# Turning w, r and k for 16 of 24 attention units on VectorE instead of TensorE

## The chip, the core and the metric

The kernel runs on one core of a Trainium2 chip. The metric is the device time of one execution in microseconds. A core has five engines that run side by side and wait for each other by semaphores: TensorE (PE, with its weight loads PEld), VectorE (DVE), ScalarE (ACT), GpSimd (POOL) and SyncE (SP), which in this kernel issues all transfers. Each engine works through its own instructions in order.

## What is computed

A linear attention with a per-channel decay, then two feed-forward layers on all 3,072 tokens. B=4 batches, H=8 heads, S=768 time steps, D=48 channels a head, all float32; the feed-forward weights come as float64.

```python
for t in range(S):
    kt, vt, rt, wt = (k[:, :, t], v[:, :, t], r[:, :, t], w[:, :, t])
    cur = np.einsum('bhd,bhe->bhde', u[None] * kt, vt)
    y[:, :, t] = np.einsum('bhd,bhde->bhe', rt, state + cur)
    state = wt[:, :, :, None] * state + np.einsum('bhd,bhe->bhde', kt, vt)
# layer 1 (384 -> 2048 -> 384)
h = x @ w_in; g = h - np.tanh(h); x = g @ w_out
# layer 2 (384 -> 1024 -> 384)
h = x @ w_in; e = np.exp(h - max(h)); sm = e / (sum(e) + 1e-9); solu = h * sm
out = ((solu - mean) / sqrt(var + 1e-6) * g_ln) @ w_out
```

## The kernel before

The attention is cut into 24 units of 128 time steps (4 batches of 6), each for all 8 heads. A unit needs r, k and w with the channels in the partitions and the time along the columns: head pair j has its even head in partitions 0 to 47 and its odd head in 64 to 111, so that one tile of 128x4x128 (j, time) holds all heads. `att_load` (L182) reads them as they lie in memory, time in the partitions, in runs of 48 floats, into `rkw`, two buffers that units take in turn; v goes into one of four `vt`. `_transposes` (L216) turns one of the three with four 128x128 transposes on TensorE into a PSUM bank.

A unit has six parts. `att_pre` (L194): ScalarE tests w against its two bounds with sums into `flags` (L198, L200), GpSimd multiplies u, r and k (L202, L203), VectorE sums them over the channels (`dg`, L204). `att_0`: transposes of w and r (L219), the running product of w by four scans on VectorE (L228), its inverse by Ln and Exp on ScalarE (L231, L232), `rh` (L233). `att_1`: transposes of k, and `kh` out of it (L240 to L242). `att_2`: the products of r and k (`qk`), masked into `aq`, and `kh` turned back. `att_3`: the state, `ds` on TensorE and L281, L282 on VectorE. `att_4`: the output `y`, split into a rounded and a remaining half (L299 to L302, into `xs` and `x3`), and six small copies from `x3` into `xs` that SyncE issues (L305).

The first layer runs in 6 blocks of 512 tokens with 16 steps each, 96 steps in all. Each step s has `part1` (nine 128x512 matmuls into `hp`, L335; then L340 to L347 on ScalarE and VectorE, L351 and L352 on GpSimd, which make `g`) and, of the step two before, `part2` (nine matmuls from `g` into three banks `x2p`, L359). Part k of unit u is put into step 4u + k - 18, so four steps carry one unit, and the four units of a block are done two steps before the block begins. `att_pre` is in step 4u - 19 and `att_load` in step 4u - 24. The first four units run ahead of the steps. The weights are converted from float64 during the first steps, and later steps read them again to test them (`check_pair`). After the last steps the second layer runs over 24 tiles of 128 tokens; there VectorE already turns data in 32x32 blocks (L473).

A scheduler gives every engine's instructions their order, from readiness in a simulated run; the code above sets the priorities. Attention takes its PSUM from a pool of three banks with the tag "a" (`bank`, L206): for w, r, k, two for qk, kt, ds and y of every unit.

Of the kernel before, what the change touches and what calls it, by code (L numbers as in the profile page):

```python
# [20 lines left out]
C = 128  # L21
NC = S // C
# [8 lines left out]
NP = 112  # L31

# [23 lines left out]
class Kern:  # L56
# [101 lines left out]
    def att_setup(self, att, xp0, xp1):  # L158
        nc = self.nc
        self.rkw = [att.tile([128, 3, H, 64], F32, name=f"rkw{i}") for i in range(2)]  # L160
# [32 lines left out]

    def att_pre(self, u):  # L194
        nc = self.nc
        t = self.rkw[u % 2]
        w = t[:, 2, :, 0:D]
        nc.scalar.activation(self.ruk, w, AF.Relu, bias=self.c_lo, scale=-1.0,  # L198
                             accum_out=self.flags[:, 2 * u:2 * u + 1])
        nc.scalar.activation(self.ruk, w, AF.Relu, bias=self.c_hi,  # L200
                             accum_out=self.flags[:, 2 * u + 1:2 * u + 2])
        nc.gpsimd.tensor_tensor(self.ruk, t[:, 0, :, 0:D], self.ub, ALU.mult)  # L202
        nc.gpsimd.tensor_tensor(self.ruk, t[:, 1, :, 0:D], self.ruk, ALU.mult)  # L203
        nc.vector.reduce_sum(self.dg[u % 2].rearrange("p e j -> p j e"), self.ruk.rearrange("p (j e) d -> p j e d", e=2), axis=AX)  # L204
# [17 lines left out]
    def att_0(self, u):  # L222
        nc, v = self.nc, self.nc.vector
        inc = self.inc[u % 2]
        pw = self._transposes(u, 2)
        pr = self._transposes(u, 0)
        for j in range(4):
            v.tensor_tensor_scan(inc[:NP, j, 1:], pw[:NP, j], self.zeros[:NP].to_broadcast([NP, C]), 1.0, ALU.mult, ALU.add)  # L228
        full = inc[:NP, :, 1:]
        kh = self.kh[u % 2]  # L230
        nc.scalar.activation(kh[:NP], full, AF.Ln, bias=self.c_min[:NP])  # L231
        nc.scalar.activation(kh[:NP], kh[:NP], AF.Exp, scale=-1.0)  # L232
        v.tensor_tensor(self.rh[u % 2][:NP], pr[:NP], inc[:NP, :, 0:C], ALU.mult)  # L233

    def att_1(self, u):
# [3 lines left out]
        pk = self._transposes(u, 1)  # L239
        self.nc.gpsimd.tensor_tensor(inv, full, kh, ALU.mult)  # L240
        v.tensor_tensor(kh, kh, pk[:NP], ALU.mult)
        v.scalar_tensor_tensor(kh, inv, 2.0, kh, ALU.subtract, ALU.mult)  # L242
# [284 lines left out]
def fast_path(tc, K, const):  # L527
# [8 lines left out]
    K.st0 = const.tile([128, 40], F32, name="st0")  # L536
# [34 lines left out]
    for s in range(-2, NB * NM + 2):  # L571
# [10 lines left out]
        if rem == 0 and UB + 1 < u < NU:  # L582
            K.att_load(u)
        if 0 <= s - 2 < NB * NM:
# [12 lines left out]
        if s == LAST + NM - 2:  # L597
# [6 lines left out]
            hs = {0: K.b_h(K.load_x2(0), 0, None, (K.st0[:, 0:8], K.st0[:, 8:40], *big))}  # L604
# [222 lines left out]
```

## Time and profile before

| what | value |
|---|---|
| median of 3 runs | 807.62 us (806.01, 807.74, 807.62) |
| the profiled execution | 804.36 us |
| its span, first to last instruction | 802.6 us |
| TensorE busy | 755.1 us (94%) |
| VectorE, ScalarE, GpSimd busy | 559.0, 499.1, 423.8 us |
| moved by DMA | 97.40 MB, mean 121 GB/s |

A busy TensorE is not a TensorE at its peak: matmuls overlap, and their ends are modelled. What an instruction costs there is read from the starts of the ones behind it. Idle time of an engine matters only where something waits for it.

### The profile page before, as it was taken

The numbers are of one execution on the slowest core, as the hardware profiler recorded it, in microseconds if no ns is written. First come the engines' busy times: TensorE is split into PE (matmuls) and PEld (weight loads), VectorE is DVE, ScalarE is ACT, GpSimd is POOL, SyncE is SP. The second block draws the span as 40 slices with busy tenths as digits, with TensorE's granted clock in tenths as the row PEclk, the third lists the DMA queues.
The fourth block names the chain that finished last, engine by engine and source line by source line (L and its number), as shares of the span: only waits on it lengthen the run. The fifth ranks groups of instructions, "written<-read, shape, count | busy, mean of one in ns | idle before, by whom it ended". The sixth has DMA issues, their size and how long they took to land. (4 is left out here: it accounts for less than half of the span.)

```text
span 802.6 us, 13281 instructions
## 1 busy us (share of the span) xinstructions
PE 755.1 (94%) x4530; PEld 626.6 (78%) x4530; DVE 559.0 (70%) x975; ACT 499.1 (62%) x944; POOL 423.8 (53%) x388
## 2 busy tenths in 40 slices
PE   3777988999999999999999999999998999999997
PEld 2666766788888888888888888776877899898886
DVE  4678979875555555565556555468559999998882
ACT  3435777786677776676767664588735555454552
POOL 3544765655565565455565555366615445445440
PEclk9979999999999999999999999999999999999999
DMA  9965576563454645354354210033035555555521
GB/s 165 175 107 126 144 162 125 149 153 87 101 125 101 146 85 123 85 154 100 97 131 142 64 46 25 32 131 118 2 121 178 169 175 169 175 166 167 188 99 46
DMA packets 167150, 97.40 MB, mean 121 GB/s; under 512 B 109088, under 2 KB 155808, under 8 KB 167072
## 3 DMA queue, kind: packets, MB, share of 16 engines
q1 hardware_dynamic: 167072, 96.45, 47.6%
q8 instruction: 38, 0.62, 0.3%
q14 instruction: 40, 0.33, 0.1%
HBM read 73.08 MB, written 20.97 MB: 117 GB/s over the span
## 5 line engine op out<-in xcount | busy, mean ns | idle before, releaser
L335 PE MATMUL hp<-xs,wa 128*128 128x512 f32 x864 | 221.9, 397 | 6.2 <-DVE y L346 2.6
L359 PE MATMUL x2p<-g,wa 128*128 128x512 f32 x864 | 223.0, 397 | 4.7 <-POOL g L352 3.1
L335 PEld LDWEIGHTS hp<-xs,wa 128*128 128x128 f32 x864 | 160.3, 189 | 43.9 <-DVE y L346 3.5
L359 PEld LDWEIGHTS x2p<-g,wa 128*128 128x128 f32 x864 | 158.2, 188 | 41.5 <-POOL g L352 6.3
L352 POOL TENSOR_TENSOR g<-y,g 128x512 fp32r<-128x512 f32 x96 | 128.7, 1341 | 43.7 <-ACT g L349 30.0
L341 DVE TENSOR_TENSOR y<-hp,t 128x512 f32<-128x512 f32 x96 | 66.1, 689 | 101.9 <-ACT t L340 95.6
L420 PE MATMUL h<-wb,x2s 128*128 128x512 f32 x432 | 107.6, 403 | 2.4 <-POOL x2s L405 2.3
L498 PE MATMUL o<-wb,ts 128*128 128x384 f32 x576 | 106.4, 339 | 0.9 <-POOL ts L477 0.9
L347 ACT ACTIVATE q<-t,cst 128x512 f32<-128x512 f32 x96 | 69.4, 723 | 59.7 <-DVE y L346 59.2
L498 PEld LDWEIGHTS o<-wb,ts 128*128 128x128 f32 x576 | 101.9, 188 | 3.3 <-POOL ts L477 1.3
L420 PEld LDWEIGHTS h<-wb,x2s 128*128 128x128 f32 x432 | 82.0, 190 | 22.2 <-POOL x2s L405 3.3
L351 POOL TENSOR_SCALAR g<-y 128x512 fp32r<-128x512 f32 x64 | 44.2, 691 | 84.8 <-DVE y L346 84.1
L340 ACT ACTIVATE t<-hp 128x512 f32<-128x512 f32 x96 | 56.8, 591 | 42.2 <-PE hp L335 42.0
L477 POOL TENSOR_TENSOR ts<-tw,ts 128x512 fp32r<-128x512 f32 x44 | 55.8, 1291 | 4.8 <-ACT ts L476 4.7
L346 DVE SCALAR_TENSOR_TENSOR y<-q,y 128x512 f32<-128x512 f32 x64 | 53.3, 833 | 5.9 <-ACT q L344 2.1
L246 POOL TENSOR_SCALAR_AFFINE_SELECT aq<-dg 128x1024 f32<-128x1024 f32 x24 | 28.4, 1182 | 39.6 <-PE y L297 36.6
L405 POOL TENSOR_TENSOR x2s<-x2s 128x384 fp32r<-128x384 f32 x24 | 24.4, 1017 | 43.9 <-ACT x2s L404 43.9
L344 ACT ACTIVATE q<-t,cst 128x512 f32<-128x512 f32 x64 | 46.3, 724 | 1.8
L451 POOL TENSOR_TENSOR st<-st,cst 128x1 f32<-128x1 f32 x24 | 13.2, 551 | 64.1 <-DVE st L450 47.4
L449 ACT ACTIVATE e<-so 128x1024 f32<-128x1024 f32 x24 | 25.4, 1059 | 33.6 <-DVE so L448 33.5
L473 DVE STREAM_TRANSPOSE tw<-sw 128x1024 f32<-128x1024 f32 x22 | 45.3, 2058 | 1.2 <-issue 0.4
L219 PE MATMUL tp<-ident,rkw 128*128 128x128 f32 x264 | 40.7, 290 | 5.7 <-DMA rkw<-in_w_dram 5.6
(120 smaller groups left out, 1218.4 us busy)
## 6 DMA issues: line engine op xcount, KB each, us to landing
raw<-in_moe_w_out_dram SPq DMA_DIRECT2D x48, 384.0 KB, 3.9
dso<-so SPq DMA_DIRECT2D x22, 512.0 KB, 3.0
sw<-dso SPq DMA_DIRECT2D x88, 128.0 KB, 3.0
raw<-in_moe_w_in_dram SPq DMA_DIRECT2D x64, 144.0 KB, 3.2
raw<-in_moe_w_in_dram SPq DMA_DIRECT2D x16, 384.0 KB, 3.2
rkw<-in_w_dram SPq DMA_DIRECT2D x24, 192.0 KB, 4.2
rkw<-in_r_dram SPq DMA_DIRECT2D x24, 192.0 KB, 4.6
rkw<-in_k_dram SPq DMA_DIRECT2D x24, 192.0 KB, 4.1
```

The costliest lines, as they stand in the source:

```text
L335: self.mm(hp, self.wa[:, a, m, j * 128:(j + 1) * 128], xs[:, b, j], start=n == 0, stop=n == len(seq) - 1)
L340: nc.scalar.activation(t, hp, AF.Square)
L341: v.tensor_tensor(y, hp, t, ALU.mult)
L344: nc.scalar.activation(p, t, AF.Square, bias=self.c_fsb, scale=F_S)
L346: self.last_dve = v.scalar_tensor_tensor(y, p, F_E, y, ALU.add, ALU.mult)
L347: self.last_act = nc.scalar.activation(q, t, AF.Relu, bias=self.c_t2, accum_out=self.flags[:, col:col + 1])
L352: g.tensor_tensor(gs[:, 1], y, gs[:, 0], ALU.subtract)
L359: self.mm(self.x2p[d], self.wa[:, a, m, sl], gs[:, b], start=m == 0 and n == 0, stop=m == NM - 1 and n == 2)
L420: self.mm(p[:, f], xs[:, a, j], w, start=q == 0, stop=q == 8)
L473: self.turned = nc.vector.transpose(x.rearrange("p k (t b) -> p b k t", b=4), sw)
L477: nc.gpsimd.tensor_tensor(ts[:, 1, k], x[:, k], ts[:, 0, k], ALU.subtract)
L498: self.mm(p, ts[:, a, k], self.wb[:, b, k, DM:], start=q == 0, stop=q == 3 * NM2 - 1)
```

## The change

From unit 8 on (TURN = 2 x UB = 8; sixteen of 24 units), w, r and k are not transposed on TensorE. `load_grp` reads each in groups of four consecutive time steps (192 floats, 768 bytes in one run) into a block buffer `grp`, with four copies of 32 partitions: partition 32g + t holds time steps 4t to 4t + 3 of every head of one parity, and the second of two groups of partitions stands 32 columns further left, so that the same column range shows channels 0 to 31 in one and 32 to 47 (with 16 unused) in the other. `turn` then lets VectorE transpose 32x32 blocks out of it into a PSUM bank, writing every fourth column, which gives the layout that the transposes gave. The block buffers are single and lie, together with a natural copy of r and k (`nat`, for `att_pre`), in the place of the two `rkw` buffers; each overlaps the next by 32 columns. `load_turned` takes the place of `att_load`, in step 4u - 21, with 15 issues in place of 4. The test of w moves from `att_pre` to `att_0` and reads the turned w in PSUM (128x512 in place of 128x384). In `att_1` an intermediate goes to the bank of k in place of `kh`. The small tile `st0` is dropped, and `ub` serves in its place.

```diff
--- before.py
+++ after.py
@@ -29,6 +29,9 @@
 NM2 = FF2 // 128
 NTT = NT // 128
 NP = 112
+RKW = 3 * H * 64
+ROW = 4 * 4 * D
+TURN = 2 * UB
 
 
 W_LO, W_HI = 0.75, 1.34
@@ -157,7 +160,10 @@
 
     def att_setup(self, att, xp0, xp1):
         nc = self.nc
-        self.rkw = [att.tile([128, 3, H, 64], F32, name=f"rkw{i}") for i in range(2)]
+        rkw = att.tile([128, 2 * 3 * H * 64 + 32], F32, name="rkw")
+        self.rkw = [x.rearrange("p (i h d) -> p i h d", i=3, h=H) for x in (rkw[:, 0:RKW], rkw[:, RKW:2 * RKW])]
+        self.grp = [rkw[:, ROW * i:ROW * (i + 1) + 32] for i in range(3)]
+        self.nat = rkw[:, 3 * ROW + 32:2 * RKW + 32].rearrange("p (i h d) -> p i h d", i=2, h=H)
         self.vt = [att.tile([128, DM], F32, name=f"vt{i}") for i in range(4)]
         self.inc = [att.tile([128, 4, C + 1], F32, name=f"inc{i}") for i in range(2)]
         self.rh = [att.tile([128, 4, C], F32, name=f"rh{i}") for i in range(2)]
@@ -191,16 +197,51 @@
             in_=self.v[b, :, sl, :].rearrange("h p d -> p h d"),
         )
 
+    def load_grp(self, i, u):
+        b, c = divmod(u, NC)
+        x = (self.k, self.r, self.w)[i][b].rearrange("(j e) (c t x) d -> e c t j (x d)", e=2, c=NC, x=4)
+        for g in range(4):
+            e, half = divmod(g, 2)
+            o = 32 - 32 * half
+            self.nc.sync.dma_start(
+                out=self.grp[i][32 * g:32 * g + 32, o:o + ROW].rearrange("p (j n) -> p j n", j=4), in_=x[e, c]
+            )
+
+    def load_turned(self, u):
+        nc = self.nc
+        b, c = divmod(u, NC)
+        sl = slice(c * C, (c + 1) * C)
+        if u == TURN:
+            nc.gpsimd.memset(self.grp[2][:, ROW:], 1.0)
+        self.load_grp(2, u)
+        self.load_grp(1, u)
+        for i, src in ((0, self.r), (1, self.k)):
+            nc.sync.dma_start(out=self.nat[:, i], in_=src[b, :, sl, :].rearrange("h p d -> p h d"))
+        nc.sync.dma_start(
+            out=self.vt[u % 4].rearrange("p (h d) -> p h d", h=H),
+            in_=self.v[b, :, sl, :].rearrange("h p d -> p h d"),
+        )
+        self.load_grp(0, u)
+
+    def turn(self, u, i):
+        p = self.bank(u, "tp")
+        x = self.grp[i][:, 32:32 + ROW].rearrange("p (j x c) -> p j x c", j=4, x=4)[:, :, :, 0:32]
+        self.nc.vector.transpose(p.rearrange("p j (t x) -> p j x t", x=4), x)
+        return p
+
+    def check_w(self, u, w, tmp):
+        for i, (b, s) in enumerate(((self.c_lo, -1.0), (self.c_hi, 1.0))):
+            self.nc.scalar.activation(tmp, w, AF.Relu, bias=b, scale=s,
+                                      accum_out=self.flags[:, 2 * u + i:2 * u + i + 1])
+
     def att_pre(self, u):
         nc = self.nc
         t = self.rkw[u % 2]
-        w = t[:, 2, :, 0:D]
-        nc.scalar.activation(self.ruk, w, AF.Relu, bias=self.c_lo, scale=-1.0,
-                             accum_out=self.flags[:, 2 * u:2 * u + 1])
-        nc.scalar.activation(self.ruk, w, AF.Relu, bias=self.c_hi,
-                             accum_out=self.flags[:, 2 * u + 1:2 * u + 2])
-        nc.gpsimd.tensor_tensor(self.ruk, t[:, 0, :, 0:D], self.ub, ALU.mult)
-        nc.gpsimd.tensor_tensor(self.ruk, t[:, 1, :, 0:D], self.ruk, ALU.mult)
+        r, k = (t[:, 0, :, 0:D], t[:, 1, :, 0:D]) if u < TURN else (self.nat[:, 0], self.nat[:, 1])
+        if u < TURN:
+            self.check_w(u, t[:, 2, :, 0:D], self.ruk)
+        nc.gpsimd.tensor_tensor(self.ruk, r, self.ub, ALU.mult)
+        nc.gpsimd.tensor_tensor(self.ruk, k, self.ruk, ALU.mult)
         nc.vector.reduce_sum(self.dg[u % 2].rearrange("p e j -> p j e"), self.ruk.rearrange("p (j e) d -> p j e d", e=2), axis=AX)
 
     def bank(self, u, name):
@@ -222,8 +263,13 @@
     def att_0(self, u):
         nc, v = self.nc, self.nc.vector
         inc = self.inc[u % 2]
-        pw = self._transposes(u, 2)
-        pr = self._transposes(u, 0)
+        if u < TURN:
+            pw = self._transposes(u, 2)
+            pr = self._transposes(u, 0)
+        else:
+            pw = self.turn(u, 2)
+            self.check_w(u, pw, self.kh[u % 2])
+            pr = self.turn(u, 1)
         for j in range(4):
             v.tensor_tensor_scan(inc[:NP, j, 1:], pw[:NP, j], self.zeros[:NP].to_broadcast([NP, C]), 1.0, ALU.mult, ALU.add)
         full = inc[:NP, :, 1:]
@@ -236,10 +282,10 @@
         v = self.nc.vector
         kh, inv = self.kh[u % 2][:NP], self.inv[:NP]
         full = self.inc[u % 2][:NP, :, 1:]
-        pk = self._transposes(u, 1)
+        pk = self._transposes(u, 1) if u < TURN else self.turn(u, 0)
         self.nc.gpsimd.tensor_tensor(inv, full, kh, ALU.mult)
-        v.tensor_tensor(kh, kh, pk[:NP], ALU.mult)
-        v.scalar_tensor_tensor(kh, inv, 2.0, kh, ALU.subtract, ALU.mult)
+        v.tensor_tensor(pk[:NP], kh, pk[:NP], ALU.mult)
+        v.scalar_tensor_tensor(kh, inv, 2.0, pk[:NP], ALU.subtract, ALU.mult)
 
     def att_2(self, u):
         nc, v = self.nc, self.nc.vector
@@ -533,7 +579,6 @@
     K.load_act_set()
     K.setup(const)
     K.gl = const.tile([128, NM2], F32, name="gl")
-    K.st0 = const.tile([128, 40], F32, name="st0")
     L, R, R2 = ExitStack(), ExitStack(), ExitStack()
     cv = pool(L, "cv", 2)
     cvr = pool(L, "cvr", 2)
@@ -579,8 +624,11 @@
         if rem == 0 and UB < u < NU:
             K.att_pre(u)
         u, rem = divmod(s - OFF + 6, 4)
-        if rem == 0 and UB + 1 < u < NU:
+        if rem == 0 and UB + 1 < u < TURN:
             K.att_load(u)
+        u, rem = divmod(s - OFF + 3, 4)
+        if rem == 0 and TURN <= u < NU:
+            K.load_turned(u)
         if 0 <= s - 2 < NB * NM:
             K.part2(*divmod(s - 2, NM), gs.pop(s - 2))
         if 0 <= s < NM - early:
@@ -601,7 +649,8 @@
                 for x in ("e0", "so0")
             ]
             K.ps_b, K.exps = (ps_r,), []
-            hs = {0: K.b_h(K.load_x2(0), 0, None, (K.st0[:, 0:8], K.st0[:, 8:40], *big))}
+            small = K.ub.rearrange("p h d -> p (h d)")
+            hs = {0: K.b_h(K.load_x2(0), 0, None, (small[:, 0:8], small[:, 8:40], *big))}
         n, due = divmod(3 * (s - NM), 7)
         if 0 <= n < NM + NM2 and due < 3:
             K.check_pair(cvr, n)
```

## Rows read from the trace of the kernel before

**Rows 1.** The page: busy time of TensorE, its 40 slices, its granted clock

```profile
PE 755.1 (94%) x4530; PEld 626.6 (78%) x4530; DVE 559.0 (70%) x975; ACT 499.1 (62%) x944; POOL 423.8 (53%) x388
...
PE   3777988999999999999999999999998999999997
...
PEclk9979999999999999999999999999999999999999
```

**Rows 2.** Stretches: length, busy PE, PEld, DVE, ACT, POOL (count), clock, DMA share, GB/s

```profile
259.10:280.40 21.30, 21.30 (x138) 17.22 (x137) 12.01 (x23) 15.92 (x33) 12.55 (x12) 1.00 0.62 154
...
302.50:324.60 22.10, 22.10 (x154) 18.10 (x153) 13.28 (x25) 15.49 (x31) 12.90 (x12) 1.00 0.52 109
...
sum 343.30, PE 343.30 PEld 281.23 DVE 203.72 ACT 237.12 POOL 198.94; mean PE 21.46 PEld 17.58 DVE 12.73 ACT 14.82 POOL 12.43
```

**Rows 3.** Timeline of TensorE in one unit: start us, us, instruction, count

```profile
307.01 1.09 PE L219 MATMUL tp<-ident,rkw 128*128 128x128 f32 x8
307.86 2.32 PE L359 MATMUL x2p<-g,wa 128*128 128x512 f32 x9
310.02 2.26 PE L335 MATMUL hp<-xs,wa 128*128 128x512 f32 x9
...
313.04 0.60 PE L219 MATMUL tp<-ident,rkw 128*128 128x128 f32 x4
313.39 1.40 PE L359 MATMUL x2p<-g,wa 128*128 128x512 f32 x5
...
322.51 2.22 PE L359 MATMUL x2p<-g,wa 128*128 128x512 f32 x9
```

**Rows 4.** Groups by line, whole run: busy us, mean ns, idle us before

```profile
L219 PE MATMUL tp<-ident,rkw 128*128 128x128 f32 x264 | 40.7, 290 | 5.7 <-DMA rkw<-in_w_dram 5.6
```

**Rows 5.** Timeline of GpSimd in the same unit

```profile
307.17 1.25 POOL L246 TENSOR_SCALAR_AFFINE_SELECT aq<-dg 128x1024 f32<-128x1024 f32 x1 [2.30 <-PE y L297]
...
316.48 1.29 POOL L352 TENSOR_TENSOR g<-y,g 128x512 fp32r<-128x512 f32 x1
```

**Rows 6.** The stretch of that unit, L219 alone

```profile
302.50:324.60 22.10, 1.69 (x12) 1.36 (x12) 1.00 0.52 109
```

**Rows 7.** Two lines of VectorE: ns shortest/median/longest, first and last start

```profile
L473 DVE STREAM_TRANSPOSE tw<-sw x22: 2024/2060/2067, 602.8 to 778.4; 128x1024 f32<-128x1024 f32 x22
...
L346 DVE SCALAR_TENSOR_TENSOR y<-q,y x64: 667/692/1583, 167.1 to 508.7; 128x512 f32<-128x512 f32 x64
```

**Rows 8.** Timeline of VectorE in the same unit; idle time before in brackets

```profile
305.36 0.74 DVE L281 TENSOR_TENSOR st<-ds,st 48x192 f32<-48x192 f32 x2 [2.64 <-PE ds L272]
...
307.50 1.47 DVE L346 SCALAR_TENSOR_TENSOR y<-q,y 128x512 f32<-128x512 f32 x1
...
314.02 0.69 DVE L241 TENSOR_TENSOR kh<-kh,tp 112x512 f32<-112x512 f32 x1
```

**Rows 9.** A check of w on ScalarE, 155 to 499 us: ns shortest/median/longest

```profile
L200 ACT ACTIVATE inv<-rkw,cst x15: 601/616/618, 164.0 to 469.2; 128x384 f32<-128x384 f32 x15
```

**Rows 10.** Groups by line: a 128x512 operation of ScalarE with a sum

```profile
L347 ACT ACTIVATE q<-t,cst 128x512 f32<-128x512 f32 x96 | 69.4, 723 | 59.7 <-DVE y L346 59.2
```

**Rows 11.** Timeline of SyncE's issues, in that unit and ahead of 424 us

```profile
310.95 3.78 SPq L305 DMA_DIRECT2D xs<-x  x6
...
317.45 0.42 SPq L320 DMA_DIRECT2D raw<-in_moe_w_out_dram  x1
...
419.25 3.99 SPq L305 DMA_DIRECT2D xs<-x  x6
```

**Rows 12.** Transfers, whole run: count, KB each, median us to landing

```profile
rkw<-in_r_dram SPq DMA_DIRECT2D x24, 192.0 KB, 4.6
```

**Rows 13.** Landing of the six x3 copies issued from 419.25 us

```profile
DMA to landing us min/median/max: 1.8/1.8/3.0
```

**Rows 14.** Timeline of TensorE at the border of 424 us

```profile
426.17 1.09 PE L335 MATMUL hp<-xs,wa 128*128 128x512 f32 x4
```

**Rows 15.** SyncE's waits, 120 to 500 us: total us, times, longest us

```profile
SPq L315 <- ACT raw L138: 44.4, 10, 7.6
```

## The prediction

> **What bounds the kernel now.** I read the page's engine totals and slices first, then a table of stretches over the steps that the change touches, then the order of instructions of one attention unit on each engine, and last the queue of SyncE and the transfers.
>
> The totals put TensorE at 94% and the slices show it full from the eighth slice on, at full clock [rows 1]. The table of stretches says it more sharply: from 155.3 us, where unit nine (index 8) begins to be transposed, to 498.6 us, TensorE is busy for 343.30 of 343.30 us at a granted clock of 1.00, while VectorE has 203.72, ScalarE 237.12 and GpSimd 198.94 us of work [rows 2]. These are the sixteen units that change. In this stretch an instruction taken off TensorE shortens the time unless something else then ends last; one added to another engine costs nothing while its chain has room.
>
> One unit takes 22.1 us. In the order of TensorE [rows 3] its w and r transposes (L219, eight of them) start at 307.01 and the next matmul at 307.86: 0.85 us. The four of k start at 313.04, the next matmul at 313.39: 0.35 us. They are pipelined, so the spacing of the starts is what they cost, 0.10 us each; the mean of 290 ns in the grouped line [rows 4] is latency and overlaps.
>
> How much room have the others? The chain of a step runs from hp (L335) over ScalarE, VectorE (L341, L346) and GpSimd (L351, L352) to part2 (L359), which TensorE runs about two steps later. In the unit shown the tightest of four is that of hp at 310.02: its g is ready at 316.48 + 1.29 = 317.77 [rows 5], and its part2 starts at 322.51 [rows 3]: 4.7 us to spare.
>
> **Off TensorE.** 12 transposes in each of 16 units: 16 x (0.85 + 0.35) = 19.2 us. Bounds: the union of the groups' busy time is 1.69 us a unit [rows 6], so at most 16 x 1.69 = 27.0 us if their tails too held up the next matmul, and nothing if another chain sets the pace. I take 19.2, since the starts show what the next matmul had to wait for.
>
> The Trainium skill (VectorE: DVE Perf Modes, The three transpose paths and Rules for kernel authors) speaks against the change: it sends a 128x128 transpose to TensorE where PSUM will do as a destination. It also gives 390 ns for one on TensorE (128x128, bf16), by which 192 would return an estimated 75 us. The starts above, 0.10 us apart, decide against that price.
>
> **Onto VectorE.** Three turns of 128x512 a unit, SBUF to PSUM. No row shows that form; nearest is L473, 2060 ns (median) for 128x1024 in SBUF [rows 7], half of which is 1.03 us. Below, 0.69 us, what other 128x512 operations take (L346's median) [rows 7]. Above, a turn that has to let a GpSimd instruction pass: L346 took 1.47 us at 307.50 beside the select of GpSimd that ran from 307.17 to 308.42 [rows 5, 8], so a 1.03 us turn behind a whole 1.29 us L352 [rows 5] might take 2.3 us. I take 1.03, the row of the same operation, steady from 2024 to 2067 ns: 3.1 us a unit, with bounds of 2.1 and 7.0. VectorE has 13.28 of 22.1 us busy [rows 2], 8.8 free; after the change it would have 16.4 of 20.9. Its cover is that free time and the 4.7 us above; without it the w and r turns alone (2.1 us) would stand in front of L341.
>
> What such a stretched instruction is, the Trainium skill says (SBUF — State Buffer, SBUF: two separate sides): VectorE and GpSimd share a port pair that one holds for a whole instruction, VectorE only with two SBUF inputs or in a two-port mode. The 1.47 us agrees. By that rule a one-input turn into PSUM stays at its own length unless it ran in such a mode, and the sum would stay as it is.
>
> **Elsewhere.** ScalarE's two checks of w go from 128x384 to 128x512: from 0.62 us [rows 9] to at most 0.72 us (a 128x512 form of L347) [rows 10], +0.2 us a unit on 15.49 us [rows 2]. They, like the scans, now wait for the turn of w, and the Ln and Exp stand behind them. L241 and L242 keep their sizes and write or read PSUM; none, beside 4.7 us. GpSimd's two products read `nat` in place of `rkw`, at equal size: none. The reuse of `ub` for small tiles is far behind its last use: none.
>
> Loads: 4 issues become 15 a unit, 11 x about 0.43 us = 4.7 us more of SyncE, which now issues for some 10 of 22 us (six x3 copies 3.8, twice five raw loads 2.2, four loads 2.0). Bytes: 576 KB of w, r and k become 1152 KB of blocks plus 384 KB natural, 960 KB more a unit, or 47 GB/s at 20.9 us. The stretch with 109 GB/s would then stand at 156, where the stretch 259.1 to 280.4 already stands (154 GB/s, share 0.62) with TensorE full [rows 2]. None, as long as loads land in time.
>
> Do they? Each block buffer is single, so its load starts when the unit before is turned. The tightest is r: it overlaps the last columns of k, so it waits for k's turn, about 315.0 (L241's place, 314.02 [rows 8], plus 1.03). SyncE has just ended six x3 copies (310.95 + 3.78) [rows 11] and has five raw loads of 0.4 us in line, until 317.9 [rows 11]; four r issues take to 319.7, landing (4.6 us, as a 192 KB load of r takes now) [rows 12] 324.3. The r turn is due at 307.01 + 20.9 = 327.9: 3.6 us early. Queued behind it on VectorE would be L341 and L346, behind these GpSimd's g, and TensorE's part2 with its 4.7 us. Cost none; above, see the third rival. Unit 8's first load needs both old buffers, so it waits for unit 7's k transposes and the landing has less lead; none, up to 4 us once, in steps that were not full.
>
> **Block borders: what is late next.** The last unit of a block ends in a chain that TensorE cannot run ahead of: y, two copies and two subtractions, six x3 copies from SyncE, then hp of the next block. At the border of 424 us the copies are issued from 419.25 to 423.24 [rows 11], the last of the six some 0.6 us before that end, and land 1.8 us after the start of their issue [rows 13]: the last at 424.4, its first use being at 426.17 [rows 14], 1.8 us to spare. TensorE now arrives 1.2 us earlier, leaving 0.6. If the turns of w and r (2.06 us) stand before the subtractions on VectorE, TensorE waits 1.5 us at each of four such borders (before steps 16, 32, 48 and 64): 6 us. If they run in VectorE's idle 2.64 us before L281 [rows 8], none: their banks and loads are ready well before. I take the half, 3 us.
>
> **Sum.** 19.2 - 3 = 16.2 us off. The profiled execution took 804.36 us (span 802.6), so 788.2; the runs' median is 807.62, 3.3 us above it, so I predict **791 us**.
>
> **Rivals.**
> *TensorE gains, but gives part back.* More than the borders: VectorE stands at a turn for a bank (three "a" banks; the bank of w is now held through its turn, two checks and four scans) or the order written for the queues comes out worse. For it, the banks also carry qk, kt, ds and y in each unit; against it, 4.7 us of room. 0.4 us lost a unit (6.4) and all 6 at the borders leave 19.2 - 12.4 = 6.8 off: 801 us; the span of the case is 795 to 806.
> *More than the sum.* The tails count too: 27.0 off, 781 us. Against it: starts are pipelined.
> *Slower: the r turn waits for its load.* VectorE is in order, so a late landing stops L341 and all behind it. It decides from 4.7 + 1.2 = 5.9 us late on each unit: one TensorE pays, the other is what it gained. For it: SyncE has stood up to 7.6 us at a raw load until ScalarE had read the one before [rows 15]. Against: with 3.6 us of lead a 7.6 us wait is 4.0 late, short of 5.9, and the ten such waits make 44.4 us, 4.4 each. At 7 us late on every unit: 16 x (7 - 5.9) = 17.6 us slower, 825 us.
> *The change does not do what it says.* If transposes only filled time in which TensorE would have waited for g, the time stays at 807 us. Against it are the 4.7 us.
>
> **How the numbers follow.** Forecast 0.55 (its own range 787 to 795: borders at none or 6 us, and a few tenths a unit), part given back 0.20, more 0.06, no change 0.05, slower 0.14. A measurement here tells some 0.2% (1.6 us) from no change. Faster by more than that 0.81, within it 0.05, slower 0.14. The range for 8 in 10 leaves out the slower case and the larger part of the case of 27 us: 785 to 808.
>
> **What would show it.** Right: TensorE still without gaps between the old 155 and 498 us, now some 325 us long, units at about 20.9 us; the turns on VectorE near 1.03 us; VectorE's wait for a load near none. Borders: waits of hp for xs of 0 to 1.5 us. Wrong: waits of VectorE's turns for a landing, of part2 for g, turns near 2 us, or SyncE's x3 copies starting later after y.

## The result, and the profile after

The changed kernel took 797.05 us (median of 4 runs, 795.77 to 800.25) against 807.46 us for the kernel before (4 runs): ratio 0.9881, 95% interval 0.9849 to 0.9913. In a later session it was 799.57 against 805.12 us, ratio 0.9914 (0.9879 to 0.9949), its 7 runs lying between 791.89 and 802.41. So it is faster, by 6 to 10 us in place of the 16 forecast: what came is the first rival, "TensorE gains, but gives part back". The profiled execution took 795.77 us (span 794.0).

The page of the changed kernel, where [rows 1] shows that of before: engine totals, TensorE's 40 slices, its granted clock in tenths.

```profile
PE 738.7 (93%) x4338; PEld 604.9 (76%) x4338; DVE 592.7 (75%) x1023; ACT 498.3 (63%) x944; POOL 418.7 (53%) x389
...
PE   3677989889999999999999999999999999999997
...
PEclk9978998999999999999999999999999999999999
```

TensorE has 192 instructions less (4530 - 4338), twelve in each of sixteen units. To see where the time went I cut both traces at the first hp matmul of steps 16 and 78 and at the start of the second layer. Step 16 opens the second block; in steps 16 to 78 lie units 9 to 23 (unit 8 is turned just ahead). The view of stretches of the kernel before; the columns are those of [rows 2].

```profile
0.00:162.03 162.03, 127.75 (x871) 100.53 (x871) 128.07 (x266) 96.89 (x187) 89.44 (x82) 0.95 0.72 143
162.03:498.64 336.61, 336.61 (x2261) 275.72 (x2260) 198.47 (x357) 231.75 (x468) 194.67 (x184) 1.00 0.45 105
498.64:577.31 78.67, 74.50 (x341) 58.38 (x339) 48.35 (x60) 60.13 (x115) 46.13 (x30) 1.00 0.21 72
577.31:802.60 225.29, 216.22 (x1062) 191.93 (x1060) 184.10 (x295) 110.29 (x176) 93.59 (x93) 0.99 0.45 147
...
228.06:270.40 42.34, 42.34 (x269) 34.47 (x268) 23.57 (x44) 29.75 (x61) 25.01 (x24) 1.00 0.52 122
```

The same view of the changed kernel:

```profile
0.00:167.09 167.09, 126.85 (x859) 99.28 (x859) 127.54 (x268) 96.55 (x188) 87.94 (x83) 0.93 0.68 143
167.09:493.70 326.61, 324.56 (x2081) 258.15 (x2080) 233.14 (x402) 232.13 (x468) 188.46 (x185) 1.00 0.61 154
493.70:571.97 78.27, 74.36 (x340) 58.41 (x339) 48.25 (x60) 60.12 (x115) 46.44 (x30) 1.00 0.22 73
571.97:794.00 222.03, 212.90 (x1062) 189.01 (x1060) 183.73 (x295) 109.51 (x176) 95.83 (x93) 1.00 0.46 149
...
293.68:314.92 21.24, 21.24 (x141) 16.88 (x140) 16.34 (x28) 14.16 (x29) 12.42 (x14) 1.00 0.54 136
...
229.99:272.48 42.49, 41.17 (x246) 32.24 (x245) 27.56 (x47) 30.71 (x64) 22.10 (x23) 1.00 0.68 169
```

Steps 16 to 78 lost 10.0 us (336.61 to 326.61), where fifteen units at 1.2 us should have lost 18. The start lost 5.1 us the other way: step 16 begins at 167.09 in place of 162.03. The second layer gained 3.3 us, though all that changed there is the place of two small tiles. Counted from its first matmul, it took 224.3 to 226.6 us in the profiles of the kernel before and its variants and 222.3 to 225.1 in those of the changed kernel and its variants, so most of the 3.3 lies within the spread. A part is a fall of the granted clock in the profile of before (0.50 for 3.4 us from 606.5 us); whether the two tiles have a share is not shown. The last two rows are a unit in the middle of a block and eight steps with a block border (28 to 35). The middle unit fell from 22.10 [rows 2] to 21.24; the eight steps with the border did not fall at all (42.34 to 42.49), though two units of transposes left them.

The new instructions were as cheap as any bound allowed, or nearly. Lines of the changed kernel (ns shortest/median/longest; first and last start): the turn, the loads of k into its block buffer (167 to 494 us) with the time to landing of all block loads there, the check of w.

```profile
L229 DVE STREAM_TRANSPOSE tp<-rkw x48: 677/718/729, 159.8 to 479.1; 128x512 f32<-128x512 f32 x48
...
L206 SPq DMA_DIRECT2D rkw<-in_k_dram x60: 311/430/2135, 169.5 to 466.2; - x60
...
DMA to landing us min/median/max: 2.0/2.6/6.0
...
L234 ACT ACTIVATE kh<-tp,cst x32: 667/687/701, 160.8 to 474.7; 128x512 f32<-128x512 f32 x32
```

What TensorE waited for in steps 16 to 78 of the changed kernel (us in total, times, longest); the kernel before has no such row there:

```profile
PE hp L381 <- DMA xs<-x: 2.0, 2, 1.3
```

So 2.0 us of the 8 that were lost are a visible wait, at block borders. The rest lies in steps in which TensorE is busy throughout. One place is seen in its order, the timeline of the unit from 293.68 us:

```profile
303.67 0.63 PE L381 MATMUL hp<-xs,wa 128*128 128x512 f32 x2
304.23 0.26 PE L317 MATMUL ds<-vt,kn 128*64 128x48 f32 x1
...
304.83 1.89 PE L381 MATMUL hp<-xs,wa 128*128 128x512 f32 x7
306.65 0.43 PE L340 MATMUL y<-rh,st 112*64 112x128 f32 x4
...
308.55 2.35 PE L405 MATMUL x2p<-g,wa 128*128 128x512 f32 x9
```

The sixteen small matmuls of ds (the first is shown) stand inside a group of hp, apart from y. In the kernel before (all units from the tenth on) and in others below they run straight into y. Read by starts, the nine of hp take 0.56 + 1.82 = 2.38 us here (303.67 to 304.23, 304.83 to 306.65), ds 0.60 and y 1.90 (306.65 to 308.55).

### The profile page after: what moved, and what is told of

Same layout as the page of the kernel before. It is cut to its first block, busy times and chain, and to the rows that moved or that the text cites. A ratio compares the mean times of both kernels' runs of the same rounds, so it can differ in the third digit from the quotient of the medians.

```text
span 794.0 us, 13215 instructions
## 1 busy us (share of the span) xinstructions
PE 738.7 (93%) x4338; PEld 604.9 (76%) x4338; DVE 592.7 (75%) x1023; ACT 498.3 (63%) x944; POOL 418.7 (53%) x389
## 5 line engine op out<-in xcount | busy, mean ns | idle before, releaser
L381 PEld LDWEIGHTS hp<-xs,wa 128*128 128x128 f32 x864 | 162.5, 191 | 49.4 <-POOL wa L135 7.9
L544 PE MATMUL o<-wb,ts 128*128 128x384 f32 x576 | 104.7, 335 | 1.0 <-POOL ts L523 1.0
L397 POOL TENSOR_SCALAR g<-y 128x512 fp32r<-128x512 f32 x64 | 39.6, 619 | 94.7 <-DVE y L392 90.9
L523 POOL TENSOR_TENSOR ts<-tw,ts 128x512 fp32r<-128x512 f32 x44 | 58.1, 1342 | 7.2 <-ACT ts L522 7.1
L392 DVE SCALAR_TENSOR_TENSOR y<-q,y 128x512 f32<-128x512 f32 x64 | 54.7, 855 | 6.7 <-ACT q L390 3.1
L135 POOL TENSOR_TENSOR wa<-cv_x,wa 128x768 fp32r<-128x768 f32 x16 | 29.4, 1834 | 41.0 <-ACT wa L134 35.2
L286 POOL TENSOR_TENSOR inv<-inc,kh 112x512 f32<-112x512 f32 x24 | 30.5, 1273 | 23.5 <-ACT kh L278 17.9
```

What stands on the lines that cost most here:

```text
L381: self.mm(hp, self.wa[:, a, m, j * 128:(j + 1) * 128], xs[:, b, j], start=n == 0, stop=n == len(seq) - 1)
L392: self.last_dve = v.scalar_tensor_tensor(y, p, F_E, y, ALU.add, ALU.mult)
L523: nc.gpsimd.tensor_tensor(ts[:, 1, k], x[:, k], ts[:, 0, k], ALU.subtract)
L544: self.mm(p, ts[:, a, k], self.wb[:, b, k, DM:], start=q == 0, stop=q == 3 * NM2 - 1)
```

## The experiments

The question: is the missing gain lost on TensorE's own side (its order, and borders that it now reaches too soon), so that taking transposes out by itself would show the loss too, or does it come with what the change adds elsewhere (turns, loads, the lines of `att_1`)? I began with the first as the theory and the second as the rival; the late start was a question of its own.

**The changed kernel again**, beside the three runs that follow.

> The changed kernel once more, beside the others on the same chip. Expected 0.985 to 0.991 of the kernel before, some 797 us; in its trace the stretch of steps 16 to 78 again some 10 us shorter than before, and the second layer as long as before within 3 us.

Measured: the 799.57 us above. In the profiled one (span 797.9) the order is that of the first, but steps 32 to 35 took 23.43 in place of 20.37 us. Its stretches around there:

```profile
240.00:253.80 13.80, 12.39 (x86) 9.54 (x84) 9.07 (x16) 8.41 (x17) 10.36 (x10) 1.00 0.65 151
253.80:260.60 6.80, 6.80 (x20) 4.97 (x19) 2.35 (x4) 2.46 (x5) 0.86 (x2) 0.50 0.85 195
```

TensorE stood 1.4 us for xs until 251.9 (12.39 busy of 13.80), and from 253.8 the granted clock is 0.50 (1.2 GHz) for 6.8 us, in which it is busy throughout and gets 20 matmuls done. So the wait at a border can cost some 3 us beyond its own length. The first profile has the same wait and no fall behind it.

**Does the first turned unit cost the start?** `TURN = 2 * UB + 1`, unit 8 left on TensorE.

> Unit 8 stays on TensorE, 9 to 23 are turned. If VectorE, which still converts weights when unit 8 is due, cannot carry its turns (theory: start), steps 12 to 16 get 2 to 4 us shorter than in the changed kernel and the time falls by 1 to 3 us, the 1.2 us of unit 8 already lost again. Rival: those steps were longer for another reason, then the time stays or rises by 1.2 us.

Measured 795.91 us (793.27 to 798.05), ratio 0.9883 (0.9861 to 0.9905); step 16 starts at 167.59, as late as with TURN = 8 (167.09). That VectorE cannot carry unit 8's turns was a theory of the late start. By it steps 12 to 15 should have become 2 to 4 us shorter; they took 25.33 us in place of 26.41. But they hold a fall of the granted clock (0.50 for 3.4 us from 149.3 us), by an estimate up to 1.7 us of their length. The total is 3.7 us below the changed kernel's 799.57, with overlapping intervals. So the run does not decide the theory.

**The place of ds.** Part 3 of a unit is put a step later, next to part 4, ahead of the step's other parts:

```diff
-        for k in (4, 0, 1, 2, 3):
-            u, rem = divmod(s - OFF - k, 4)
+        for k, at in ((3, 4), (4, 4), (0, 0), (1, 1), (2, 2)):
+            u, rem = divmod(s - OFF - at, 4)
```

> Part 3 of a unit is put into the step of part 4, so that on TensorE the 16 small matmuls of ds stand right ahead of y again, as before the change. Theory (order): ds and y apart cost TensorE 0.2 us in each of 13 turned units, so 2 to 3 us less than the changed kernel. Rival (the loss is waiting for other engines): no difference beyond 1 us.

Measured 798.99 us (797.17 to 801.76), ratio 0.9926 (0.9905 to 0.9948). The stretch of its middle unit:

```profile
298.20:319.12 20.92, 20.92 (x142) 16.88 (x140) 15.26 (x28) 13.33 (x29) 11.96 (x13) 1.00 0.65 156
```

The same unit's order on TensorE:

```profile
310.39 0.26 PE L317 MATMUL ds<-vt,kn 128*64 128x48 f32 x1
...
312.76 2.34 PE L405 MATMUL x2p<-g,wa 128*128 128x512 f32 x9
```

With ds beside y the unit takes 20.92 us: from 22.10 that is 1.18, the whole 1.2 of the transposes. So inside this unit the order cost 0.32 us, and the starts say where: ds and y together take 2.37 us (310.39 to 312.76) in place of 2.50, and an unbroken group of nine takes 2.20 us (297.51 to 299.71 in the last kernel below) in place of 2.38; 0.13 and 0.18 make 0.31. On the total I was wrong: the same edit moved the early units too (step 16 starts at 169.26), and the border at step 32 got worse (44.7 us for its eight steps, a wait of hp for xs of 2.3 us until 255.7, the granted clock at 0.50 behind it for 3.4 us).

**TensorE alone.** In the kernel before, one transpose of the four stays from unit 8 on; the other heads read its result. Nothing is turned on VectorE, loads are as before.

```diff
-        for j in range(4):
+        n = 4 if u < 2 * UB else 1
+        for j in range(n):
...
-        return p
+        return p if n == 4 else p[:, 0:1].to_broadcast([128, 4, C])
```

> The kernel before, from unit 8 on with one of four transposes for each of w, r and k, its result read for all four head pairs (so outputs differ). No turns, no new loads. 16 x 9 x 0.10 = 14.4 us off TensorE. Theory (borders and order, both on TensorE's side of the change): part is lost as in the changed kernel, 798 to 801 us, with waits of hp for xs at the borders. Rival (turns on VectorE and loads are what cost): nearly all arrives, 792 to 795 us.

Measured 794.86 us (793.08 to 795.93), ratio 0.9875 (0.9856 to 0.9894). Steps 16 to 78 and the middle unit:

```profile
161.99:485.75 323.76, 323.76 (x2127) 261.18 (x2125) 203.20 (x358) 230.12 (x470) 192.17 (x186) 1.00 0.45 109
...
287.76:308.91 21.15, 21.15 (x145) 17.08 (x144) 13.67 (x25) 15.32 (x31) 12.54 (x12) 1.00 0.41 88
```

Nine transposes a unit left and 12.9 us came, of 15 x 0.9 = 13.5; the middle unit fell by 0.95 of 0.9, and the start did not move. A transpose costs TensorE 0.096 us (12.9 / 135). Here I had put theory and rival the other way round: I expected most of the loss on TensorE's own side, and that fell; what is lost comes with the other edits. One transpose of each four still stands in its place here, so this is not quite the order that TensorE has with all twelve gone. The Trainium skill's price of 390 ns (VectorE: DVE Perf Modes, The three transpose paths; for bf16) would have given an estimated 53 us; the measurement decides against it for transposes that follow each other.

**The two lines of `att_1` in the kernel before**, all units:

```diff
-        v.tensor_tensor(kh, kh, pk[:NP], ALU.mult)
-        v.scalar_tensor_tensor(kh, inv, 2.0, kh, ALU.subtract, ALU.mult)
+        v.tensor_tensor(pk[:NP], kh, pk[:NP], ALU.mult)
+        v.scalar_tensor_tensor(kh, inv, 2.0, pk[:NP], ALU.subtract, ALU.mult)
```

> The kernel before with one line pair of the change alone: in att_1 the product of kh and k goes to the bank of k, for all units. Theory (start): it holds that bank through GpSimd's product, the order of the first steps becomes another, and step 16 comes some 4 to 5 us later than in the kernel before, steps 16 to 78 as before: 809 to 812 us, ratio 1.004 to 1.006. Rival (the new loads are what makes the start longer): no difference beyond 1 us.

Measured 808.85 against 804.97 us, ratio 1.0047 (1.0031 to 1.0062). Its stretches up to step 16 and from there to step 78:

```profile
0.00:165.87 165.87, 128.89 (x871) 101.57 (x872) 126.11 (x265) 96.65 (x188) 88.97 (x83) 0.93 0.70 140
165.87:502.52 336.65, 336.65 (x2262) 275.79 (x2261) 201.22 (x357) 230.88 (x467) 186.61 (x184) 1.00 0.45 105
```

Two lines that neither add nor remove an instruction cost 3.9 us by the medians, and in the profiles 3.8 us before step 16 (162.03 to 165.87); behind it the length is that of before, 336.65 against 336.61. The loss lies in steps 8 to 11:

```profile
111.37:144.59 33.22, 28.39 (x152) 21.85 (x151) 24.45 (x50) 21.61 (x41) 17.83 (x13) 0.90 0.58 134
```

In the kernel before these four steps take 29.05 us, at a granted clock of 1.00. Here it is 0.50 for 6.8 us from 120.3 us. The bank of k is now held until the second line, and the order of the early units is another one from the first of them on. Which of these it is was not separated.

**The same lines put back in the changed kernel.**

> The changed kernel with that line pair as it was before, for all units. Theory (start): step 16 comes at 162 to 164 us in place of 167, a unit of the middle still takes 21.2 us; 791 to 794 us, ratio 0.981 to 0.985. Rival (the loads): step 16 stays at 166 to 168 us, 796 to 800 us.

Measured 795.27 us (792.05 to 799.05), ratio 0.988 (0.9853 to 0.9908): a miss, or not to be told from the changed kernel. Step 16 starts at 165.15, 1.9 us earlier than in the changed kernel; the stretch behind 147.8 shows the granted clock at 0.50 for 6.8 us, so that the start cannot be read cleanly here.

**Without the six copies of x3** from unit 8 on (the changed kernel; 96 of the 384 input channels of a block keep old values):

```diff
-                nc.sync.dma_start(out=xs[dst:dst + 16, :, j, cols].bitcast(F32), in_=x3[src:src + 16].bitcast(F32))
+                if u < 2 * UB:
+                    nc.sync.dma_start(out=xs[dst:dst + 16, :, j, cols].bitcast(F32), in_=x3[src:src + 16].bitcast(F32))
```

> The changed kernel without the six x3 copies of units 8 to 23 (so outputs differ). Theory (borders): hp waits for nothing at the borders before steps 32, 48 and 64, eight steps around each take 41.5 to 42.0 us in place of 42.5 to 45.6, no fall of the clock after them: 3 to 6 us less than the changed kernel, ratio 0.983 to 0.987. Rival (the borders are slower for the order on TensorE alone): within 1 us of the changed kernel.

Measured 789.70 us (787.05 to 792.07), ratio 0.9802 (0.9782 to 0.9822):

```profile
170.42:492.25 321.83, 321.83 (x2081) 257.61 (x2080) 232.10 (x401) 231.55 (x465) 188.36 (x184) 1.00 0.58 151
```

Steps 16 to 78 go without a gap and are 4.8 us shorter (326.61 to 321.83). All of it lies at the borders: the eight steps around those before steps 32, 48 and 64 take 40.14, 42.23 and 42.19 us in place of 42.49, 43.23 and 43.58, and the other steps 197.27 in place of 197.31, with ds in the same places. The same edit in the kernel before, with the same channels left out:

> The kernel before without the x3 copies of units 8 to 23 (so outputs differ), against the changed kernel without them. Theory (borders): in the kernel before the copies stood in nobody's way up to step 78, so steps 16 to 78 take 336 to 337 us as with them; only the last border and the steps behind it get shorter, by 3 to 4 us. Rival (copies cost the same in both kernels): steps 16 to 78 get 4 to 5 us shorter too.

Measured 801.23 us (798.22 to 802.45), ratio 0.993 (0.9906 to 0.9954):

```profile
164.16:500.84 336.68, 336.68 (x2262) 275.71 (x2261) 199.29 (x356) 231.35 (x467) 195.38 (x184) 1.00 0.41 100
```

In the kernel before the copies cost nothing in these steps (336.68 against 336.61); what it gains comes behind step 78, at the last border. So at the three borders of these steps the copies are wholly hidden in the kernel before and cost 4.8 us in the changed one.

**Which edit delays the border?** The block buffers and the natural copy are loaded for unit 8 alone, later units turn the old data; v is still loaded.

```diff
-        self.load_grp(2, u)
-        self.load_grp(1, u)
-        for i, src in ((0, self.r), (1, self.k)):
+        if u == TURN:
+            self.load_grp(2, u)
+            self.load_grp(1, u)
+        for i, src in ((0, self.r), (1, self.k)) if u == TURN else ():
...
-        self.load_grp(0, u)
+        if u == TURN:
+            self.load_grp(0, u)
```

> The changed kernel with the block loads and the natural loads of r and k for unit 8 alone, later units reading its data (so outputs differ): 14 issues and 1.5 MB a unit left out. Theory (loads are hidden): a unit of the middle 21.2 us as in the changed kernel, the borders up to 1 us shorter each, the time 0 to 4 us less. Rival (loads or SyncE's issues are what costs): 0.4 us or more less in every unit, over 7 us in all.

Measured 795.51 us (793.03 to 797.63), ratio 0.9855 (0.9824 to 0.9887). The middle unit, steps 16 to 78, and the eight steps with the border at step 32:

```profile
294.89:316.13 21.24, 21.24 (x142) 16.88 (x140) 15.11 (x26) 14.69 (x30) 13.07 (x13) 1.00 0.20 51
169.85:494.18 324.33, 324.33 (x2081) 257.85 (x2080) 233.95 (x401) 231.07 (x466) 188.12 (x185) 1.00 0.29 82
232.76:273.71 40.95, 40.95 (x245) 32.05 (x244) 28.60 (x49) 30.82 (x65) 22.19 (x23) 1.00 0.39 111
```

Inside a unit the loads are hidden to the last digit (21.24 with and without). At the borders they are not: the eight steps around the three take 40.95, 43.27 and 42.81 us in place of 42.49, 43.23 and 43.58, and of the 4.8 us of all borders 2.3 are theirs (326.61 to 324.33). With no loads no hp waits for xs.

**The turns doubled**, every `v.transpose` issued twice.

> The changed kernel with each turn done twice: 3 x 0.72 = 2.2 us a unit more on VectorE, for 16 units 35 us. Theory (VectorE's turns are hidden): a unit of the middle 21.2 to 21.5 us, at most 5 us more in all. Rival (VectorE sets the pace): 1 to 2 us a unit more, 16 to 35 us in all.

Measured 803.79 us (795.19 to 804.26, and one of 809.84 that is not in the ratio), ratio 0.9969 (0.9944 to 0.9993). The profiled execution was the shortest of them. Its middle unit:

```profile
290.88:311.81 20.93, 20.93 (x142) 16.88 (x140) 17.46 (x31) 15.91 (x32) 12.52 (x13) 1.00 0.53 132
```

Inside a unit three turns more cost nothing; the scheduler here happened to set ds beside y, hence 20.93. On the whole the medians are 4 to 7 us above the changed kernel's, on either side of the 5 I had set as a limit; the one wait of its TensorE in steps 16 to 78 is again of hp for xs, 2.8 us at a border. Steps 16 to 78 take 325.07 us there, 1.5 less than in the changed kernel. Where the longer executions lose time no profile shows.

**Three repairs together**: the old lines of `att_1`, ds beside y, and at a block's first unit `rh` and the turn of k ordered behind the subtraction that the copies wait for.

> The changed kernel with three edits: the line pair of att_1 as before, part 3 in the step of part 4, and at a border VectorE's rh and turn of k behind the subtraction into x3. By the theories on order, start and borders 16 to 19 us less than the kernel before: 787 to 790 us, ratio 0.976 to 0.980; a unit of the middle 20.9 us, waits of hp for xs under 1 us at each border. If only the order counts, 0.988.

Measured 798.58 us (797.06 to 799.09), ratio 0.9915 (0.99 to 0.993): a miss by 9 us. No hp waits for xs any more and steps 16 to 78 take 323.58 us, but step 16 starts at 170.00, 8 us later than in the kernel before. The moved ds had changed the early units as well; that this is the cause is not shown by itself.

**The same with the early units left alone**: TURN = 9, ds moved only for the turned units.

```diff
-TURN = 2 * UB
+TURN = 2 * UB + 1
...
-        for k in (4, 0, 1, 2, 3):
-            u, rem = divmod(s - OFF - k, 4)
-            if rem == 0 and UB <= u < NU:
+        for k, at in ((3, 4), (4, 4), (0, 0), (1, 1), (2, 2), (3, 3)):
+            u, rem = divmod(s - OFF - at, 4)
+            if rem == 0 and UB <= u < NU and (k != 3 or (at == 4) == (u >= TURN)):
...
+    def behind(self, u):
+        return self.tc.issue_after(self.halved.ins) if u >= TURN and u % UB == 0 else nullcontext()
...
-        pk = self._transposes(u, 1) if u < TURN else self.turn(u, 0)
+        with self.behind(u):
+            pk = self._transposes(u, 1) if u < TURN else self.turn(u, 0)
...
-        v.tensor_tensor(pk[:NP], kh, pk[:NP], ALU.mult)
-        v.scalar_tensor_tensor(kh, inv, 2.0, pk[:NP], ALU.subtract, ALU.mult)
+        v.tensor_tensor(kh, kh, pk[:NP], ALU.mult)
+        v.scalar_tensor_tensor(kh, inv, 2.0, kh, ALU.subtract, ALU.mult)
```

> Three edits as in the run before, but the first steps left as they were in the kernel before: unit 8 on TensorE, turned units from 9, part 3 moved to part 4's step from unit 9 on only, the line pair of att_1 as before. TensorE's order is the old one through step 17. Theory (order, start, borders): step 16 at 161 to 164 us, a unit of the middle 20.9 us, 15 units x 1.2 = 18 us less a little at the borders: 788 to 791 us, ratio 0.979 to 0.983. Rival (the start is longer for the new loads): step 16 at 166 us or later, 793 us or more.

Measured 792.33 us (790.16 to 794.34) against 805.96, ratio 0.983 (0.9804 to 0.9857): faster than the kernel before, and a little above what I expected. The changed kernel has 0.9881 and 0.9914; the interval of the first just overlaps with this one. The start, steps 16 to 78, and the middle unit:

```profile
0.00:161.97 161.97, 127.70 (x870) 99.23 (x871) 128.97 (x266) 96.89 (x187) 89.46 (x83) 0.91 0.73 144
161.97:485.88 323.91, 323.35 (x2082) 257.87 (x2080) 231.51 (x402) 229.23 (x468) 190.54 (x184) 1.00 0.61 154
...
287.51:308.43 20.92, 20.92 (x141) 16.88 (x140) 15.60 (x30) 12.07 (x26) 10.28 (x11) 1.00 0.61 146
```

The start is that of the kernel before (161.97 against 162.03), the middle unit has its 1.18 us. The eight steps around the borders take 42.47, 43.52 and 42.09 us, without a wait for xs. The third is 1.5 us shorter than in the changed kernel and as short as without any copies (42.19). The first two are as long as in the changed kernel; ahead of step 32 y is broken into pieces between the matmuls of x2p. With ds moved alone the second and third took 41.95 and 41.89 us. Why the first two stay long here is open.

**The start, over all the profiles.** Up to step 16 TensorE has the same order of groups (runs of matmuls into one tile) in the changed kernel and in four of the runs above: the same again, without copies, loads left out, turns doubled. Yet step 16 starts at 167.09, 166.80, 170.42, 169.85 and 162.79 us in these five. The order of the kernel before is also that of its variants with one transpose and without copies, and of the last kernel: 162.03, 161.99, 164.16 and 161.97 us. So the 5.1 us are one pair out of two spreads. What is steady is steps 12 to 15, 25.6 to 30.1 us in the first five and 21.5 to 22.2 in the other four. The kernel before and the changed one there, and what TensorE of the changed one waited for:

```profile
139.94:162.03 22.09, 21.14 (x137) 16.35 (x136) 19.46 (x40) 15.88 (x30) 13.51 (x10) 1.00 0.60 142
...
140.68:167.09 26.41, 22.05 (x139) 17.19 (x137) 21.56 (x44) 17.76 (x34) 13.35 (x11) 1.00 0.69 169
...
PE hp L381 <- POOL wa L135: 2.7, 2, 2.4
PE qk L301 <- DVE cv_x L131: 1.6, 1, 1.6
```

The 4.3 us are the length of its waits for the conversion of the weights (L131, L135), of which the kernel before has none there. In steps 8 to 11, where the two lines of `att_1` alone cost 4.2 us, the changed kernel took 29.83 us against 29.05. So the two lines do not cost there what they cost in the kernel before, and their 3.8 us cannot simply be set against the 5.1.

## Why the prediction was right in direction and 6 us too low

Its terms against the profiled executions (802.6 to 794.0 us, 8.6 off):

| term | predicted | came |
|---|---|---|
| transposes off TensorE | -19.2 | -18.0 in steps 16 to 78 (15 units) |
| block borders | +3 | +4.8 |
| order of the matmuls in a unit | 0 (0.4 a unit in the first rival) | +3.2 (the rest: 8.0 less 4.8) |
| up to step 16 | 0 (unit 8's 1.2 stands in the first row) | +5.1 |
| steps 78 to 95, second layer | 0 | -0.4, -3.3 (mostly spread) |

*TensorE is the bound, and a transpose costs the spacing of its starts.* Right: 0.096 us against 0.10, and 0.95 and 1.18 us a unit where the rest was held still. The tails (27.0 us) paid nothing.

*The turns on VectorE.* Right that they are hidden, mis-sized in their length: 0.718 us, not 1.03. The nearest row was not that of the same operation (2060 ns for 128x1024 within SBUF) but the lower bound, what other 128x512 operations take. VectorE still came to 16.34 us a unit, near the 16.4 forecast. That is luck: other work was stretched by about as much as the turns were shorter, above all the pair that ends the state (L328, L282 before). The changed kernel's VectorE, and that of before:

```profile
305.88 1.46 DVE L328 TENSOR_TENSOR st<-st,inc 48x192 f32<-48x192 f32 x2
...
311.22 1.53 DVE L392 SCALAR_TENSOR_TENSOR y<-q,y 128x512 f32<-128x512 f32 x1
...
306.74 0.73 DVE L282 TENSOR_TENSOR st<-st,inc 48x192 f32<-48x192 f32 x2
```

All 48 turns lie between 677 and 729 ns, though 31 of them ran beside an instruction of GpSimd, while a two-input operation of the same size reached 1.53 us. This agrees with the rule of the Trainium skill (SBUF — State Buffer, SBUF: two separate sides) by which an instruction with one SBUF input, outside a two-port mode, has no need of the pair of ports that VectorE and GpSimd share.

*The loads, and the slower rival.* Right inside a unit: no turn waited for a landing (nor for a bank, as the first rival had it), and leaving the loads out moves the unit by nothing. But "SyncE's 15 issues: none, as long as loads land in time" was the wrong question. At the border SyncE is a queue on the path. SyncE and TensorE of the changed kernel there:

```profile
245.20 0.85 SPq L206 DMA_DIRECT2D rkw<-in_r_dram  x2
246.09 1.85 SPq L206 DMA_DIRECT2D rkw<-in_k_dram  x4
248.05 4.48 SPq L351 DMA_DIRECT2D xs<-x  x6
...
252.11 0.93 PE L381 MATMUL hp<-xs,wa 128*128 128x512 f32 x3 [1.32 <-DMA xs<-x]
```

The last subtraction ended at 245.96 (245.69 + 0.27, L348), and the copies could go; they were issued 2.1 us later, behind the block loads, and TensorE then stood 1.32 us. That is the mechanism that I had costed at nothing.

*The borders.* I took 3 us between none and 6, for turns of w and r ahead of the subtractions; 4.8 came, of which 2.3 vanish with the loads. The other part is partly what I named: at the border behind 413 us, ScalarE and VectorE of the changed kernel:

```profile
413.31 0.46 ACT L345 CAST xs<-y 112x384 fp32r<-112x384 f32 x1
...
414.67 0.71 DVE L229 STREAM_TRANSPOSE tp<-rkw 128x512 f32<-128x512 f32 x1
415.29 0.67 DVE L392 SCALAR_TENSOR_TENSOR y<-q,y 128x512 f32<-128x512 f32 x1
415.88 0.53 DVE L347 TENSOR_TENSOR xs<-y,xs 112x384 fp32r<-112x384 f32 x1
```

The subtraction L347 has its input at 413.77 (413.31 + 0.46) and starts at 415.88, behind a turn, but that of k, and behind L392. Ordering `rh` and this turn behind the subtractions took the waits away, and yet the first two borders stayed long: naming the wait was not the whole of the cost. That the third came down to 42.09 us is not shown to be the work of the ordering either, since with ds moved alone it took 41.89. So what a border costs hangs on the place of ds too, and the table's 4.8 and 3.2 are not independent of each other.

*The start* was put at nothing but for "up to 4 us once", for unit 8's first load. The 4.7 us against which L241 and L242 were put at nothing are the room of a unit in the middle of a block; the two lines are in all 24 units. In the kernel before they cost 3.9 us by themselves, in steps 8 to 11. That shows the step to be wrong, but the loss of the changed kernel lies in steps 12 to 15, where TensorE waits for converted weights. VectorE, which takes part in that conversion, has 2.1 us more work in these steps (19.46 to 21.56), about the three turns of unit 8, which were not set against this work. With unit 8 left on TensorE alone, and with the old lines alone, these steps took 25.33 and 25.92 us, each with a fall of the granted clock in them; with both, 22.16. No run separates turns, loads, lines and the new order of TensorE: the cause of the late start is open.

*The order of ds.* The sum held the order of TensorE's other instructions fixed while taking twelve out. The first rival named a worse order, at 0.4 us a unit, without saying where. The scheduler set ds apart from y: of the thirteen units with a ds in steps 16 to 78, twelve run it straight into y in the kernel before and none in the changed one. Besides the unit looked at, the cost can be read in steps 68 to 77, which hold two units, in the changed kernel and in the last one:

```profile
441.58:493.70 52.12, 52.12 (x333) 41.51 (x332) 34.97 (x62) 32.33 (x64) 28.00 (x28) 1.00 0.30 80
...
434.45:485.88 51.43, 51.43 (x334) 41.40 (x332) 37.32 (x63) 31.75 (x64) 29.76 (x29) 1.00 0.33 89
```

That is 0.69 us for two units. In these steps and in steps 36 to 43 (42.45 us in the changed kernel) the five kernels that have ds ahead of y there are 0.60 to 0.69 us shorter for two units. In these four units ds splits a group of hp; in the other eight it splits a group of x2p, which was not priced. Twelve times 0.3 would be 3.6, near the 3.2 that are left.

*The spread.* The changed kernel's runs spread over 10 us on one chip, those of before over 4 (803.43 to 807.18, 12 runs); the fall of the clock behind a border wait, in one profile and not in another, is about 3 us of it, and the start, between 162.79 and 170.42 us with the same order on TensorE, up to 7.6.

## What to carry to other kernels

Read the cover of an edit at every place that it touches: the room in the steady state says nothing of the first units, where TensorE still waits for other engines. Where one stretch of a kernel varies from execution to execution, as the start does here, compare several profiles before a difference there is given a cause. For each transfer on a path, list what the issuing queue will have to issue ahead of it, not only whether the new loads land in time. And when instructions are taken from a full engine under a scheduler, look at the new order first: small matmuls that are set apart can cost more than their rows say.

## What the runs showed of the hardware that was not expected

A 128x512 turn in 32x32 blocks from SBUF into PSUM took 0.718 us; one of 128x1024 within SBUF takes 2.06 [rows 7], so 1.4 times the time per element. After a wait of TensorE of 1.4 us the granted clock was 0.50 for 6.8 us in one execution and 1.00 in another of the same kernel. Sixteen 128x48 matmuls inside a group of nine 128x512 ones cost 0.32 us more than the same sixteen ahead of y (0.13 on ds and y, 0.18 on the group of hp that they split), and 0.30 to 0.35 in each of four units where it could be read.
